# A second feed-forward product by one level of Strassen, with sums on GpSimd and three weight combinations streamed from DRAM

## The chip, the core and the metric

The kernel runs on one core of a Trainium2 chip. The metric is the device time in microseconds, as the median of several executions. A core has TensorE (PE; its weight loads, PEld, are listed apart), VectorE (DVE), ScalarE (ACT), GpSimd (POOL) and SyncE (SP), whose queue issues nearly all DMAs here. Each engine works through its instructions in the order of the program and waits on semaphores for the others.

## What is computed

An attention in which each query keeps its 32 largest scores, and behind it a feed-forward block, all in float32:

```python
# q, k, v: (8, 8, 576, 64); w_in: (512, 2048); w_out: (2048, 512)
scores = q @ k^T / 8
mask   = scores >= (the row's 32nd largest score)
attn   = softmax of the masked scores
x      = (attn @ v) with heads side by side     # 4608 tokens x 512
h      = x @ w_in
g      = h - tanh(h)
out    = g @ w_out                              # 4608 x 512
```

## The kernel before

**Attention.** A step handles two heads of one batch and a tile of 128 queries. Each batch has 16 such steps, and two more for the last 64 queries of each head; there are 144 steps in all. In step n, these parts of different steps run beside each other:

- `scores(n + 1)`: PE makes the scores in PSUM (L267), ACT copies them to SBUF (L275).
- `search(n)`: DVE finds the 32 largest (L297 to L319).
- `mask(n - 1)`: POOL makes the threshold `tb` (L334), ACT a Relu (L347), POOL a subtraction (L350) and flags (`bad`, L354). `expo(n - 1)`: ACT's exponential (L370), and POOL's small `rd` (L380).
- `invert(n - 2)` and `divide(n - 2)`: after the first round of the search, DVE's reciprocal (L389) and ACT's scaling (L396). `turn_z(n - 2)`: DVE transposes 32x32 blocks into `zx` when the search is done (L427).
- `spread_keys(n - 2)`, in steps whose pair of query tiles is complete (every second one): SP issues one DMA from `zx` to DRAM (`there`, L442), waits until it has landed and issues four DMAs back (`et`, L444).
- `values(n - 5)`: PE multiplies with v (L492), ACT copies the result to `xT` (L512).

The first batch (`pe`) transposes on PE instead, while the weights arrive in pieces and are converted on DVE, ACT and POOL.

**Feed-forward.** Tokens are gathered in units: 256 tokens (two query tiles of one batch), except 128 at the start of batch 0, and "rest" units of 128 tokens from two batches' last queries. `ffn(u)` cuts a unit into items. A full unit has 16 items `ffn_h` (256 columns times one block of 128 of `w_in`, four accumulated matmuls, L543; after every second item ACT makes tanh and a copy, L555 and L556, and POOL subtracts, L557) and 16 items `ffn_o` (two matmuls of 512 columns against `w_out`, L564; after eight of them ACT copies 128 tokens' output, L574, and SP stores it, L576). In the profile a float32 matmul is two records. A PSUM bank of `h_ps` holds 512 columns; there are two.

**The order.** The program is written out by hand. `rate()` computes how many items a step should take so that work lasts until the next unit is ready; `deal(part)` puts that share of them in place. A step's order, cut to what matters:

```python
mask(n - 1, exact)
search(n, exact, between)       # with invert, divide and turn_z of n - 2
spread_keys(n - 2)              # if steps[n - 2].last
deal(0.4)
due()                           # values
scores(n + 1)
expo(n - 1)
deal(0.2); deal(0.2)
for fn in todo.pop(n, []): fn() # loads of q, k, v
deal(0.2)
```

So SP meets a DMA that an item issues behind everything that the program issued on SP before it, the waits of `spread_keys` included.

Of the kernel before, what the change touches and what calls it, by code (L numbers as in the profile page):

```python
# [19 lines left out]
J = 4  # L20
# [5 lines left out]
class Step:  # L26
# [3 lines left out]

    def __init__(self, b, hp, qt, unit, col, i=0, nq=1, pe=False):
        self.b, self.hp, self.qt, self.unit, self.col = b, hp, qt, unit, col
        self.i, self.nq, self.pe = i, nq, pe
        self.rem = qt == J
        self.last = i == nq - 1

        self.lag = 2 if pe else LAG


class Unit:  # L40
# [3 lines left out]
    def __init__(self, blocks, tag):  # L44
        self.blocks, self.tag = blocks, tag
        self.n = 128 * len(blocks)
        self.xT = None
        self.g = []
# [3 lines left out]
def kernel(  # L52
# [46 lines left out]
    thpool = pool("th", 4)  # L99
    gpool = pool("g", 4)  # L100
    dpool = pool("d", 2, space=bass.MemoryType.DRAM)
    sc_ps = pool("sc_ps", 1, space=PS)
    zt_ps = pool("zt_ps", 2, space=PS)
    h_ps = pool("h_ps", 2, space=PS)

# [14 lines left out]
    et2 = [consts.tile([P, 4 * S], FP32, name="et")[:], later[:, 0 : 4 * S]]  # L120
    et_rem = later[:, 4 * S : 6 * S]
    e896 = consts.tile([P, 1], FP32, name="e896")
    nc.gpsimd.memset(e896[:], -896.0 * 2.0**23)
# [16 lines left out]
    def convert(piece, slot):  # L140
# [19 lines left out]

        e = h_ps.tile([P, NW], FP32, tag="h", name="e")[:] if j < WJ else f[:]
        nc.scalar.activation(e.bitcast(I32), fu, AF.Relu, bias=e896[:], scale=2.0**23)
# [14 lines left out]

    raw, kT, qT, vb, vr = {}, {}, {}, {}, {}

# [9 lines left out]

    def load_rows(name, b, hp, exact):  # L190

        if b == 0 and hp and not exact:
            x = early[2 * hp - 2 + (name == "q")]
        else:
            x = ldpool.tile([P, S], FP32, tag=f"{name}in", name=f"{name}in")[:]
        raw[name, b, hp] = x
        src = {"k": k, "q": q}[name]
        if b == 0 and hp and not exact:

            xv = x.rearrange("p (c t d) -> p t c d", t=2, d=D)  # L200
            for t in range(2):
                h = 2 * hp + t
                nc.sync.dma_start(
                    xv[:, t, 0:J, :], src[b, h, 0:JP, :].rearrange("(c p) d -> p c d", p=P)
                )
                nc.sync.dma_start(xv[0:R, t, J, :], src[b, h, JP:S, :])
            return
        for a in range(NG):
            h, d = 2 * hp + a // 2, a % 2 * G
            queue = nc.scalar if a and (name, b, hp, exact) == ("q", 0, 0, False) else nc.sync  # L210
            queue.dma_start(
                x[a * G : (a + 1) * G, :].rearrange("i (n d) -> i n d", d=G),
                src[b, h, :, d : d + G].rearrange("(n i) d -> i n d", i=G),
            )

    def load_v(b, hp):


        x = vb[b, hp] = kqpool.tile([P, 2, J, D], FP32, tag="vb", name="vb")
        y = vr[b, hp] = vrs[hp]  # L220
        for t in range(2):
            h, o = 2 * hp + t, t * R
            nc.sync.dma_start(
                x[:, t, :, :], v[b, h, o : o + JP, :].rearrange("(c p) d -> p c d", p=P)
            )
            o = 0 if t else JP
            nc.sync.dma_start(y[half(t), t, :], v[b, h, o : o + R, :])

    turned_pe = [True]

    def turn_rows(name, b, hp):

        d = kqpool.tile([P, S], FP32, tag=f"{name}T", name=f"{name}T")
        {"k": kT, "q": qT}[name][b, hp] = d
        x = raw.pop((name, b, hp))
        if not (b == 0 and hp and turned_pe[0]):
            nc.vector.transpose(d[:], x)  # L237
            return
# [19 lines left out]
    def scores(n):  # L258
        g = steps[n]
        ps = sc_ps.tile([P, 2, 2, 512], FP32, tag="sc", name="scps")  # L260
        for s in range(2):
            ks = slice(s * S2, (s + 1) * S2)
            for i in range(2 if g.rem else 1):
                qs = slice(JP, S) if g.rem else slice(g.qt * P, (g.qt + 1) * P)
                rows = half(i) if g.rem else slice(0, P)
                for t in range(2):
                    nc.tensor.matmul(  # L267
                        ps[rows, t, s, 0:S2],
                        qT[g.b, g.hp + i][half(t), qs],
                        kT[g.b, g.hp + i][half(t), ks],  # L270
# [128 lines left out]

    rxs = {}  # L400

    def spread(n):

        if steps[n].last:
            rd = rds.pop(n)
            nq = steps[n].nq
            rx = rxs[n] = xpool.tile([P, 2, 2, D], FP32, tag="rx", name="rx")
            nc.gpsimd.tensor_copy(
                rx[:, 0:nq], rd[:, 0:nq].unsqueeze(3).to_broadcast([P, nq, 2, D])
            )  # L410

    zxs, ets, last_et = {}, {}, [0]

# [18 lines left out]
    def spread_keys(n):  # L432
# [4 lines left out]
        if not rem:  # L437
            last_et[0] ^= 1
        et = ets[n] = et_rem if rem else et2[last_et[0]]
        w = steps[n].nq * S // 2  # L440
        there = dpool.tile([P, NG * w], FP32, tag=f"there{steps[n].nq}", name="there")
# [36 lines left out]
    def values(n):  # L478
# [7 lines left out]
        for i in range(2 if g.rem else 1):  # L486
# [3 lines left out]
            for c in range(J + 1):  # L490
                for t in range(2):
                    nc.tensor.matmul(  # L492
                        av[half(t), 0, cols],
                        vb[g.b, hp][:, t, c, :] if c < J else vr[g.b, hp][:, t, :],
                        es[:, :, (J + 1) * t + c if c < J else J].rearrange("p a i j -> p a (i j)"),
# [3 lines left out]
        if g.pe:  # L499
            rx = rxs.pop(n)  # L500
            for i in range(nq):
                nc.tensor.transpose(
                    in_order(av[:, 1, 0:w], nq)[:, i], rx[:, i].rearrange("p t d -> p (t d)"), ident[:]
                )
            xs = xrpool.tile([P, 2, N], FP32, tag="xs", name="xs")
            nc.scalar.copy(xs[:, :, 0:w], av[:, :, 0:w])
# [26 lines left out]
    def ffn_h(u, item):  # L533
# [3 lines left out]
        for f in range(item * per, (item + 1) * per):  # L537
            j, fo = f // FJ, (f % FJ) * P
            s = f * w % 512
            if s == 0:  # L540
                cur[u] = h_ps.tile([P, 512], FP32, tag="h", name="hps")
            for c in range(CD):
# [7 lines left out]
        if item % 2:  # L550
            th = thpool.tile([P, 512], FP32, tag="th", name="th")
            if item % 4 == 1:
                u.g.append(gpool.tile([P, 2, 512], FP32, tag="g", name="g"))
            g = u.g[-1][:, item % 4 // 2, :]
            nc.scalar.activation(th[:], cur[u][:], AF.Tanh)  # L555
# [3 lines left out]
    def ffn_o(u, i, part):  # L559
        if part == 0:  # L560
            cur[u] = h_ps.tile([P, DM], FP32, tag="h", name="ops")
        for f in range(2 * part, 2 * part + 2):
            o = f * u.n + i * P
            nc.tensor.matmul(  # L564
                cur[u][:],
                u.g[o // 1024][:, o % 1024 // 512, o % 512 : o % 512 + P],
                w_out[f // FJ][:, f % FJ, :],
# [7 lines left out]
        for rows, dst in u.blocks[i]:  # L575
            nc.sync.dma_start(dst, ot[rows, :])  # L576

    def ffn(u):

        nh = CF * u.n // (2 * P)  # L580
        for item in range(nh):
            f = (item + 1) * CF // nh - 1
            yield CD * (f // FJ + 1), u, lambda item=item: ffn_h(u, item)
        for i in range(len(u.blocks)):
            for part in range(CF // 2):
                yield CD * (WJ + part // 2 + 1), None, lambda i=i, part=part: ffn_o(u, i, part)

# [4 lines left out]
    def plan():  # L592
# [6 lines left out]
        for b in range(B):  # L599
            if b % 2 == 0:  # L600
                rest = Unit(
                    [[(half(i), out[(b + i) * S + JP : (b + i + 1) * S, :]) for i in range(2)]], "xTr"
                )
# [4 lines left out]
            for a, qts in enumerate(parts):  # L608
                unit = Unit([block(b, qt) for qt in qts], "xT")
                pe = b == 0  # L610
                for hp in range(NHP):
                    for i, qt in enumerate(qts):
                        steps.append(Step(b, hp, qt, unit, 0, i, len(qts), pe))
                    if hp == NHP - 1:
                        done[len(steps) - 1] = unit
                    if hp % 2 and a == (0 if b == B - 1 else len(parts) - 1):
                        steps.append(Step(b, hp - 1, J, rest, b % 2 * R, pe=pe))
                        if hp == NHP - 1 and b % 2:
                            done[len(steps) - 1] = rest
# [7 lines left out]
    def run(exact):  # L627
        plan()
        turned_pe[0] = not exact
        NS = len(steps)  # L630
        todo, at_round, turned = {}, {}, {}
# [4 lines left out]

        pairs = [(b, hp) for b in range(B) for hp in range(NHP)]
        for i, (b, hp) in enumerate(pairs):
            n = next(n for n, g in enumerate(steps) if (g.b, g.hp) == (b, hp))
            for x, name in enumerate("kq"):  # L640
                m = max(n - 5 + x, turned.get(name, -4))
                if b == 0 and not exact:
                    m = -4
                at(m, lambda x=(name, b, hp, exact): load_rows(*x))
                if x and i < NHP and not exact:
                    at(-4, lambda: load_piece())
                turn = lambda x=(name, b, hp): turn_rows(*x)
                if 0 < i < NHP:
                    at_round.setdefault((n - 1, 0), []).append(turn)
                    turned[name] = n - 1  # L650
                else:
                    at(n - 3 + x, turn)
                    turned[name] = n - 3 + x
            at(n + 1 if b else n - 1, lambda b=b, hp=hp: load_v(b, hp))

# [15 lines left out]
        def part(x, k):  # L671
            next(loaded[k][0])
            if x == 2:
                converted[0] = k + 1
                free.append(loaded[k][1])
                load_piece()
# [47 lines left out]
        def rate():  # L724


            have, low, high = len(work), 0.0, None
            coming = sorted((t, u.n // 8) for u, t in ready.items() if t > n)
            for t, k in coming + [(NS + LAG, 0)]:
# [108 lines left out]
```

## Time and profile before

| | |
|---|---|
| Median of three executions | 1509.0 us (1508.56 to 1510.21) |
| The profiled execution | 1509.65 us |
| Its span, first to last instruction | 1507.5 us |
| Mean granted TensorE clock | 0.982 |
| PE busy | 1426.5 us (95%), 7332 records |
| DVE busy | 1295.2 us (86%) |
| ACT busy | 1004.9 us (67%) |
| POOL busy | 879.1 us (58%) |
| DMA | 221.68 MB, queue of SP at 56.0% of 16 engines' time |

Busy times are unions over the span. The slices of the page cut the span into 40 equal parts; a digit is the busy share in tenths. The chain of waits follows the work that ended last back through what released it. In a group, the number behind the bar is its busy time, then the mean duration of one instruction, then the engine's idle time before them and what ended it.

### The profile page before, as it was taken

The numbers are of one execution on the slowest core, as the hardware profiler recorded it, in microseconds if no ns is written. First come the engines' busy times: TensorE is split into PE (matmuls) and PEld (weight loads), VectorE is DVE, ScalarE is ACT, GpSimd is POOL, SyncE is SP. The second block draws the span as 40 slices with busy tenths as digits, with TensorE's granted clock in tenths as the row PEclk, the third lists the DMA queues.
The fourth block names the chain that finished last, engine by engine and source line by source line (L and its number), as shares of the span: only waits on it lengthen the run. The fifth ranks groups of instructions, "written<-read, shape, count | busy, mean of one in ns | idle before, by whom it ended". The sixth has DMA issues, their size and how long they took to land.

```text
span 1507.5 us, 25020 instructions
## 1 busy us (share of the span) xinstructions
PE 1426.5 (95%) x7332; PEld 908.2 (60%) x7332; DVE 1295.2 (86%) x4886; ACT 1004.9 (67%) x1813; POOL 879.1 (58%) x1370
## 2 busy tenths in 40 slices
PE   4667898999999999999999999999999999999998
PEld 2454656465666565656565665657575675656673
DVE  7999899999998999999989999899988989886100
ACT  4766777777776777777676676768676676766220
POOL 3777667566565575657565575747474664646120
PEclk9888999999999999999999999999999999999999
DMA  9954123657854685567655865466554766443400
GB/s 277 373 170 167 25 43 92 171 156 153 205 147 140 164 166 156 134 176 171 162 136 146 175 147 165 138 166 159 156 145 117 174 144 177 111 140 105 109 7 17
DMA packets 248563, 221.68 MB, mean 147 GB/s; under 512 B 190816, under 2 KB 197984, under 8 KB 241248
## 3 DMA queue, kind: packets, MB, share of 16 engines
q1 hardware_dynamic: 246640, 219.75, 56.0%
q8 instruction: 61, 1.00, 0.3%
q14 instruction: 86, 0.70, 0.2%
q10 hardware_dynamic: 1776, 0.22, 0.1%
HBM read 136.17 MB, written 83.76 MB: 146 GB/s over the span
## 4 chain that ended last, share of the span: by engine, by line
PE 74%; DVE 15%; ACT 4%; POOL 2%; DMA 2%; issue 1%; SPq 0%; ACTq 0%; DVEq 0%; POOLq 0%
PE ops L564 28%; PE hps L543 28%; PE av L492 9%; PE scps L267 8%; DVE m L316 3%; DVE top L309 2%; DVE rest L319 2%; DVE zx L427 2%; DVE ab L303 1%; DMA w_in<-in_k_dram 1%; DVE f L170 1%; PE zt L464 1%; DVE f L159 1%; DVE top L319 1%; DVE ab L298 1%
## 5 line engine op out<-in xcount | busy, mean ns | idle before, releaser
L564 PE MATMUL ops<-w_out,g 128*128 128x512 f32 x1152 | 517.5, 600 | 2.4 <-POOL bad L354 1.5
L543 PE MATMUL hps<-xT,w_in 128*128 128x256 f32 (+1 forms) x2176 | 466.7, 372 | 1.0 <-ACT g L556 0.9
L350 POOL TENSOR_TENSOR z<-sc,z 128x576 f32<-128x576 f32 x288 | 404.5, 1426 | 86.2 <-ACT z L347 86.2
L543 PEld LDWEIGHTS hps<-xT,w_in 128*128 128x128 f32 x2176 | 392.0, 192 | 75.8 <-issue 21.6
L564 PEld LDWEIGHTS ops<-w_out,g 128*128 128x128 f32 x1152 | 213.3, 191 | 262.3 <-issue 250.3
L347 ACT ACTIVATE z<-sc,tb 128x576 f32<-128x576 f32 x288 | 207.6, 769 | 141.9 <-POOL tb L334 141.2
L557 POOL TENSOR_TENSOR g<-g,th 128x512 f32<-128x512 f32 x144 | 183.6, 1277 | 145.7 <-ACT g L556 140.9
L396 ACT ACTIVATE z<-z,rd 128x576 f32<-128x576 f32 x252 | 180.7, 764 | 97.0 <-DVE rd L389 96.9
L370 ACT ACTIVATE z<-z,nb 128x576 f32<-128x576 f32 x288 | 221.6, 774 | 2.5 <-POOL z L350 2.4
L380 POOL TENSOR_SCALAR rd<-den 128x2 f32<-128x2 f32 x144 | 32.7, 227 | 312.9 <-ACT z L370 307.1
L267 PE MATMUL scps<-kT,qT 64*128 64x288 f32 (+1 forms) x1280 | 189.0, 447 | 18.4 <-DVE qT L237 8.2
L427 DVE STREAM_TRANSPOSE zx<-z 128x1152 f32<-128x1152 f32 x126 | 172.0, 1365 | 35.2 <-ACT z L396 34.6
L309 DVE MAX8 top<-ab 128x8 f32<-128x144 f32 x864 | 194.6, 295 | 0.0
L275 ACT COPY sc<-scps 128x1152 f32<-128x1152 f32 x144 | 160.4, 1114 | 41.8 <-PE scps L267 41.4
L316 DVE MAX8 m<-rest 128x8 f32<-128x168 f32 x576 | 161.6, 322 | 0.0
L267 PEld LDWEIGHTS scps<-kT,qT 64*128 64x128 f32 (+1 forms) x1280 | 102.4, 184 | 94.5 <-issue 19.9
L316 DVE MAX8 m<-top 128x8 f32<-128x144 f32 (+1 forms) x576 | 151.7, 305 | 0.0
L555 ACT ACTIVATE th<-hps 128x512 f32<-128x512 f32 x144 | 84.2, 585 | 64.5 <-PE hps L543 62.1
L303 DVE TENSOR_TENSOR ab<-scps,sc 128x576 f32<-128x576 f32 x144 | 107.6, 748 | 0.0
L297 DVE TENSOR_TENSOR scps<-scps,sc 128x288 f32<-128x288 f32 x144 | 64.6, 449 | 46.1 <-ACT sc L275 45.7
L354 POOL TENSOR_SCALAR bad<-top,tb 128x3 uint8<-128x3 f32 x288 | 95.0, 341 | 0.0
L492 PE MATMUL av<-et,vb 128*64 128x256 f32 (+1 forms) x640 | 76.8, 372 | 18.2 <-ACT et L467 18.2
(78 smaller groups left out, 1536.8 us busy)
## 6 DMA issues: line engine op xcount, KB each, us to landing
there<-zx SPq DMA_DIRECT2D x56, 1152.0 KB, 4.2
spare<-there SPq DMA_DIRECT2D x112, 288.0 KB, 4.7
et<-there SPq DMA_DIRECT2D x112, 288.0 KB, 5.2
kin<-in_k_dram SPq DMA_DIRECT2D x116, 72.0 KB, 2.9
vb<-in_v_dram SPq DMA_DIRECT2D x64, 128.0 KB, 5.9
out_dram<-ot SPq DMA_DIRECT2D x32, 256.0 KB, 3.3
qin<-in_q_dram SPq DMA_DIRECT2D x113, 72.0 KB, 3.7
there<-zx SPq DMA_DIRECT2D x14, 576.0 KB, 5.2
```

The lines of the kernel that those rows point to most:

```text
L267: nc.tensor.matmul(ps[rows, t, s, 0:S2], qT[g.b, g.hp + i][half(t), qs], kT[g.b, g.hp + i][half(t), ks], start=True, stop=True,)
L309: nc.vector.max(top[:, t, o : o + 8], low[:, t, i, :])
L316: nc.vector.max(m[:, t, m8], seen[i][t])
L347: nc.scalar.activation(zv[:, t, :], scf[:, t, :], AF.Relu, bias=tb[:, t : t + 1], scale=-BIG)
L350: nc.gpsimd.tensor_tensor(zv[:, t, :], scf[:, t, :], zv[:, t, :], ALU.subtract)
L370: nc.scalar.activation(x["zv"][:, t, :], x["zv"][:, t, :], AF.Exp, bias=x["nb"][:, t : t + 1], scale=scale, accum_out=den[:, t : t + 1],)
L396: nc.scalar.activation(x, x, AF.Copy, scale=rds[n][:, g.i, t : t + 1])
L427: nc.vector.transpose(tiles(zx, g.nq)[:, :, :, g.i, :].rearrange("p c k j -> p k c j"), z[:].rearrange("p (k c j) -> p k c j", c=NG, j=G),)
L492: nc.tensor.matmul(av[half(t), 0, cols], vb[g.b, hp][:, t, c, :] if c < J else vr[g.b, hp][:, t, :], es[:, :, (J + 1) * t + c if c < J els ...
L543: nc.tensor.matmul(cur[u][:, s : s + w], w_in[j][:, c, fo : fo + P], u.xT[:, c, 0:w], start=(c == 0), stop=(c == CD - 1),)
L557: nc.gpsimd.tensor_tensor(g, g, th[:], ALU.subtract)
L564: nc.tensor.matmul(cur[u][:], u.g[o // 1024][:, o % 1024 // 512, o % 512 : o % 512 + P], w_out[f // FJ][:, f % FJ, :], start=(f == 0), sto ...
```

## The change

For a full unit, the second product becomes one level of Strassen's method in Winograd's form. With A the unit's 256 x 2048 `g` cut into 2 x 2 quarters (128 tokens by every second 128-block of the inner dimension) and B `w_out` cut likewise (1024 by 256), seven products of 128 x 1024 x 256 replace eight.

- **Products.** An item `ffn_p` is one half of a product's inner dimension: four matmuls of 256 columns. A full unit has 16 items `ffn_h` and 14 `ffn_p`, 30 instead of 32. Even products go to one PSUM bank, odd ones to the other, and accumulate there; after each product ACT copies 256 columns out, and the next product but one goes into the same place.
- **Sums.** Four sums of `g` quarters for each half of the inner dimension (eight of 128x512 elements) and three joins of outputs (128x256) a unit are made on POOL.
- **Weights.** Four combinations T1 to T4 for each of four parts of `w_out` are made once on POOL, two in each of the first eight items of the first full unit. B11, B22, T1 and T2 stay in SBUF. B21, T3 and T4 lie in DRAM (`kept`) and are streamed for each unit through `flow`, two buffers of 512 KB, one for each half of the inner dimension.
- **Other tiles.** To make room, q is loaded for each half of the query tiles, v is loaded twice a batch with three buffers instead of four, and several tiles share `more`.
- **Rest units** gather four batches' last queries (256 tokens) instead of two's, and so become full units.

The core of the diff:

```diff
+    ORDER = [("A11", "B11"), ("A12", "B21"), ("S2", "T2"), ("S3", "T3"), ("S1", "T1"), ("A22", "T4"), ("S4", "B22")]
+    FLOW = ["B21", "T3", "T4"]
+
+    def stream(i):
+        x, k = FLOW[i // 2], i % 2
+        nc.sync.dma_start(flow[k], kept[x][:, 4 * k : 4 * k + 4, :])
+
+    def sum_up(u, k, x):
+        (a11, a12), (a21, a22) = quarters(u, k)
+        s1, s2 = sums[k]
+        out_, a, b, op = [
+            (s1, a21, a22, ALU.add),
+            (s2, s1, a11, ALU.subtract),
+            (a21, a21, a11, ALU.subtract),
+            (a12, a12, s2, ALU.subtract),
+        ][x]
+        nc.gpsimd.tensor_tensor(out_, a, b, op)
...
+    def product(u, i, k):
...
+        acc = cur[u][i % 2][:, 0 : 2 * P]
+        fresh = i in (0, 1, 3)
+        for m in range(4):
+            if right in FLOW:
+                rhs = flow[k][:, m, :]
...
+            nc.tensor.matmul(acc, lhs[:, m, :], rhs, start=(fresh and k == 0 and m == 0), stop=(k == 1 and m == 3), skip_group_check=True)
+        return acc
+
+    def ffn_p(u, item):
+        i, k = item // 2, item % 2
+        acc = product(u, i, k)
...
+        if item in (3, 4):
+            sum_up(u, item - 3, 3)
+        if item < 3:
+            sum_up(u, 1, item)
+        if ORDER[i][1] in FLOW[:-1]:
+            stream(2 * FLOW.index(ORDER[i][1]) + 2 + k)
+        if not k:
+            return
+        if i == 0:
+            u.y = pair("oy")
+            nc.scalar.copy(u.y[:, lo], acc)
+        elif i == 1:
+            u.o0 = pair("ot")
+            nc.scalar.copy(u.o0[:, lo], acc)
+            join(u.o0[:, lo], u.y[:, lo])
...
+    def ffn_full(u, item):
+        ffn_h(u, item)
+        if item in (6, 7):
+            stream(item - 6)
+        if combined[0] < 4 * WJ:
+            for _ in range(2):
+                combine(combined[0] // 4, combined[0] % 4)
+                combined[0] += 1
+        if 8 <= item < 11:
+            sum_up(u, 0, item - 8)
...
-    gpool = pool("g", 4)
+    gpool = pool("g", 2)
...
-    h_ps = pool("h_ps", 2, space=PS)
+    h_ps = pool("h_ps", 1, space=PS)
...
-            if b % 2 == 0:
+            if b % 4 == 0:
                 rest = Unit(
-                    [[(half(i), out[(b + i) * S + JP : (b + i + 1) * S, :]) for i in range(2)]], "xTr"
+                    [
+                        [(half(i), out[(b + k + i) * S + JP : (b + k + i + 1) * S, :]) for i in range(2)]
+                        for k in (0, 2)
+                    ],
+                    "xTr",
                 )
...
-            at(n + 1 if b else n - 1, lambda b=b, hp=hp: load_v(b, hp))
+            at(n + 3 if b else n - 1, lambda b=b, hp=hp, part=part: load_v(b, hp, part))
```

## The prediction

> **What bounds the kernel now.** I read the page's busy shares and slices first, then the end of the chain of waits, the groups by form, and last the waits of the DMA queue.
>
> ```profile
> span 1507.5 us, 25020 instructions
> ...
> PE 1426.5 (95%) x7332; PEld 908.2 (60%) x7332; DVE 1295.2 (86%) x4886; ACT 1004.9 (67%) x1813; POOL 879.1 (58%) x1370
> ...
> PE   4667898999999999999999999999999999999998
> ...
> DVE  7999899999998999999989999899988989886100
> ...
> POOL 3777667566565575657565575747474664646120
> ```
>
> From the eleventh slice on PE is full, and it works 110 us longer than DVE: PE sets the end. It idles 1507.5 - 1426.5 = 81 us, nearly all in the first 300 us. But DVE is close behind: between 200 and 450 us the windows give it 246 of 250 us. There PE (242) waits for DVE.
>
> ```profile
> 581.67 7.06 PE ops L564 x16
> ...
> 592.21 7.10 PE hps L543 x32
> ...
> 1445.12 27.82 PE hps L543 x128
> 1472.95 27.48 PE ops L564 x64
> ```
>
> These are pieces of the chain (start, length, records). A 512-column record of the second product takes 7.06/16 = 0.441 us, a 256-column record 7.10/32 = 0.222: half the columns, half the time. So one item of the planner (4 records of 512 or 8 of 256) is 1.77 us of PE.
>
> ```profile
> SPq L444 <- DMA there<-zx: 274.3, 70, 5.3
> SPq L442 <- DVE zx L427: 242.0, 37, 18.4
> ```
>
> ```profile
> 748.89 0.34 SPq L442 DMA_DIRECT2D there<-zx  x1
> 753.11 1.76 SPq L444 DMA_DIRECT2D et<-there  x4
> 754.97 0.38 SPq L576 DMA_DIRECT2D out_dram<-ot  x1
> ```
>
> ```profile
> 737.86 5.35 PE ops L564 x12
> 743.20 1.73 PE hps L543 x8
> 744.93 1.17 PE scps L267 x8
> 746.10 7.10 PE hps L543 x32
> ```
>
> First two waits of SP's queue (us in total, times, longest), then its timeline, then the chain over the same time. SP issues in program order. In every second step it stands at L442 until DVE has turned zx, at the end of a search, then about 4 us at L444 until `there` has landed. The store of this block was ready when its last product ended, at 743.20 (plus the copy); it left at 754.97, 11.8 us later, when PE was five items on.
>
> **The change, part by part.**
>
> *Products.* 17 units of 256 tokens (14, one in batch 0, two rests) replace 64 records x 0.441 = 28.2 us by 7 x 8 x 2 = 112 records x 0.222 = 24.9. The two 128-token units keep 14.1 each. 36 x 14.1 = 508 becomes 17 x 24.9 + 28.2 = 451: -57. The first product of the rests goes from 128 columns (7.34 us for 64 records, 0.115 each; 512 of them, 59) to 256 columns (256 x 0.222 = 57): -2. Together **-59** on the path: from 300 us on PE has 12 us of idle time, so PE time counts one to one.
>
> The Trainium skill's page "TensorE: Matmul & The Clock Gate" (Part 3, The mechanism) says that a weight load overlaps running matmuls only if its row group differs. The trace differs: 128 records with 128x128 loads of 0.192 us follow each other every 0.217 us. By the page 48 more loads a unit would cost 9.2 us a unit and the change would lose 100 us on PE alone; the row decides.
>
> *Sums on GpSimd.* Each unit adds 8 x 1.277 us (row g<-g,th, the same 128x512) and three joins of 256 columns at 0.729 (row xT<-xs): 12.4 us. POOL goes from 879 to 879 + 17 x 12.4 + 16 x 1.28 (weight combinations) = 1110 us of about 1400, 79%. It lies beside PE, but in POOL's order: behind a sum wait tb, z and rd of the attention, behind these ACT's Relu and, at its end, the score copy that DVE's next search needs. From tb to the end of the next score copy lie 0.3 + 2 x 0.77 (Relu) + 2 x 0.76 (division) + 1.11 = 4.5 us, so tb may start 8.8 - 4.5 = 4.3 us after DVE's step; the timeline has it at 2 to 3 in the mean. A step gets 12.4/8.5 = 1.5 us more POOL work; part falls into the 2.1 us a step that POOL now waits for rd (307 us in all). Cost between 0 and 0.5 us in each of the 55 DVE-bound steps, 28 us; I take +5, since slack remains.
>
> *The 16 combinations* come in eight items of the first full unit, two each: 20 us of POOL where the windows give it 34 to 40 of 50 already. Up to +20, down to 0; I take +10.
>
> *Rests over four batches.* Their items come at batch 4 and batch 8 instead of after each second batch. By the planner's rule the steps 20 to 75 get about 3.15, later 3.4 items instead of 3.4 and 3.75; with 2.5 us of scores and values PE needs 8.2 and 8.5 us a step where DVE's step is 8.78. PE idles 0.6 x 25 + 0.25 x 31 = 23 us there against 11 now: up to +12, 0 if other stalls lie in the same place. +5.
>
> *Split q and repeated v loads*: 28 more transposes at 0.11 us (737 ns for 576 elements, 1365 for 1152) are 3 us of DVE: +1. The some 130 q and 56 v DMAs are on SP, which is the next point. Seven copies of 0.367 for two of 0.574 add 1.4 us a unit to ACT at 67%: nothing.
>
> *Streams.* `flow` has one buffer for each half of the inner dimension. T3's half may be issued only when product item 2 (or 3) has read B21's, and is needed at item 6 (7); T4's follows item 6 (7) and is needed at 10 (11). So from release to need PE has three items, 5.3 us, and one set of scores (1.2) or scores and values (3.5): 6.5 to 8.8 us, 7.7 in the middle. In that time SP must come to the DMA and 512 KB must land. Landing: 3.7 us (w_out, 512 KB) to 6.3 (stores issued right behind et); 4.6 is the middle (spare, 512 KB). How late SP comes is what the stores show, issued in the same deals: of the 29 between 289 and 1344 us the delays from last matmul to issue are 15.0, 9.0, 8.7, 7.1, 0.6, 0.6, 2.5, 6.5, 7.3, 1.7, 10.7, 1.8, 11.8, 0.6, 10.5, 3.7, 11.0, 9.1, 7.7, 2.5, 10.5, 8.8, 0.6, 12.2, 3.5, 3.9, 10.2, 8.0, 0.6: 6.4 in the mean, 14 over 7.5, 12 under 4. In the example above, a stream in the store's place would land at 754.97 + 4.6 = 759.6 and be needed two items after 746.10, at 749.7: 9.9 us of PE standing. Over the 29 delays, max(0, delay + 4.6 - 7.7) is 3.9 us in the mean; 15 units lie among steps with such transposes, two hand-overs each: 30 x 3.9 = 116.
>
> A second way: half of the steps turn zx, and 0.4 of the items are dealt ahead of the scores; the first deal of such a step holds one of a hand-over's two halves in about a third of the cases, 10 of 30, at some 8.5 us; some 12 fall into its later deals (SP 5 us late, 1.5 us of stall), the rest cost nothing: 103. A PE stall isn't regained: it delays the scores, thus DVE, thus SP by as much, and the lag is there again. It fills idle time where DVE binds, so I take **+95**; bounds 30 (landing 3.7, only the ten) and 150 (landing 6.3).
>
> The skill's page "DMA: Bandwidth & Descriptors" (Anatomy of one DMA) fits 2.0 us + bytes/436 GB/s, 3.2 us for 512 KB, for GpSimd's queue. No row here is as short for this size; by it the streams would cost about 30 us less.
>
> *Other new waits*: product i + 2 waits for ACT's copy of product i (3.55 us later at least; ACT now starts a tanh 1.2 us after its bank in the median, 3.6 at the 95th percentile), and item 1 for the last g (3.6 us in the median, 3.1 us of PE before it): +6, between 0 and 20.
>
> **Sum.** 1507.5 - 59 + 5 + 10 + 5 + 1 + 95 + 6 = 1570.5 us of span. The profiled execution took 1509.65, 2.15 more than its span and 0.65 above the median of 1509.0: 1570.5 + 2.15 - 0.65 = 1572.
>
> **The rivals.** (1) *Streams in time, faster*: the 12 stores under 4 us speak for it, and DMA queues that are 56% busy; the longer half of the delays speaks against. Then 1509 - 59 + 27 = 1477. It decides where stalls stay under 59 - 27 = 32 us, 1.1 us a hand-over. Chance 0.18, 1450 to 1500. (2) *GpSimd sets the pace*: ACT's 141 us of waits for tb speak for it, 21% of free POOL time against. Streams in time, 55 steps at 9.3 instead of 8.78: 1477 + 28 - 5 = 1500, spread 1490 to 1520. Chance 0.10. With late streams it is the upper end of my forecast. (3) *No gain in the products* since 256-column records don't run at half time: excluded by the chain's rows as far as they go; it is in the upper end too.
>
> **Numbers.** Forecast (late streams): 0.72, 1500 to 1650 for itself. About 3 us (0.2%) can be told from no change. Faster 0.18 + 0.02 of (2) + 0.01 of the forecast's lower edge = 0.21; same 0.03; slower 0.76. The range reaches down into the first rival, to 1488, and up to 1632 (1572 plus 55 for the streams' upper bound and 5 of the other terms): some 0.12 below, 0.07 above.
>
> **What would show it.** Right: PE busy near 1367 but the span up; in the waits, the product line on PE waiting for flow's DMA, 60 to 140 us in some 20 to 35 places, up to 12 us each; DVE idle more, on ACT's score copy; POOL about 1110 us; product records near 0.222 us in the chain. Wrong: those waits under 30 us in all; or PE waiting for POOL's sums instead; or SP's issue of flow within 3 us of the product that frees it.

## The result, and the profile after

The changed kernel takes 1724.9 us (1722.9 to 1728.9, four executions) against 1509.6 for the kernel before, run beside it: a ratio of 1.1425, 95% interval 1.1396 to 1.1454. The direction of the forecast held, its size did not: +215 us instead of +63, and outside the range. The page of the changed kernel, with the lines that answer to those shown of before, and with the granted clock:

```profile
span 1724.6 us, 27027 instructions
...
PE 1440.0 (83%) x7892; PEld 1085.6 (63%) x7892; DVE 1299.3 (75%) x4914; ACT 1017.6 (59%) x1898; POOL 1103.7 (64%) x1573
...
PE   4677986896987979797969798979796988788998
...
DVE  7998977989797979797968878779696886684000
...
POOL 4776787676584857575757656767666584756434
PEclk9788998899898989898989999989898999899999
...
PE 29%; DVE 24%; DMA 16%; ACT 14%; POOL 10%; issue 4%; SPq 2%; DVEq 0%; ACTq 0%; POOLq 0%
```

Before, the rows of the clock and of the chain were:

```profile
PEclk9888999999999999999999999999999999999999
...
PE 74%; DVE 15%; ACT 4%; POOL 2%; DMA 2%; issue 1%; SPq 0%; ACTq 0%; DVEq 0%; POOLq 0%
```

PE is no longer full from the eleventh slice on: nines and sevens alternate. Its idle time went from 81 to 1724.6 - 1440.0 = 285 us. DVE dips in the same slices. The clock, at nine tenths or more in before from the fifth slice to the end, now loses a tenth in every second or third slice; the mean is 0.925 instead of 0.982. In the chain of waits PE held 74% of the span; now it holds 29%, and DMA 16% instead of 2%.

The waits of PE (us in total, times, longest):

```profile
PE hy L721 <- DMA more<-keptT: 132.5, 23, 12.7
PE scps L329 <- DVE top L367: 37.5, 13, 12.2
...
PE hps L607 <- ACT g L620: 15.8, 12, 2.7
PE hx L721 <- POOL g L621: 8.6, 7, 3.2
```

and of SP's queue:

```profile
SPq L508 <- DMA there<-zx: 282.2, 70, 6.5
SPq L506 <- DVE zx L490: 207.1, 33, 15.1
...
SPq L701 <- PE hy L721: 84.2, 20, 29.3
```

The first line is the forecast's main wait: products (L721) stand for T3 and T4 (`more<-keptT`). One of these hand-overs in the timeline of PE (start, length, engine, line, names, records; in brackets the idle time before it and what ended it):

```profile
593.47 3.72 PE L721 MATMUL hy<-more,g 128*128 128x256 f32 x16
597.02 3.82 PE L721 MATMUL hx<-w_out,more 128*128 128x256 f32 x16
600.77 1.95 PE L556 MATMUL av<-et,vb 128*64 128x256 f32 x16
602.55 0.60 PE L556 MATMUL av<-et,vr 128*64 128x256 f32 x4
603.08 1.24 PE L329 MATMUL scps<-kT,qT 64*128 64x288 f32 x8
611.04 5.42 PE L721 MATMUL hy<-more,g 128*128 128x256 f32 x16 [6.72 <-DMA more<-keptT]
```

and in that of SP's queue over the same time:

```profile
597.50 0.35 SPq L506 DMA_DIRECT2D there<-zx  x1
602.07 1.74 SPq L508 DMA_DIRECT2D spare<-there  x4
603.91 0.85 SPq L701 DMA_DIRECT2D more<-keptT  x2
604.81 0.97 SPq L276 DMA_DIRECT2D vb<-in_v_dram  x2
605.88 5.80 SPq L259 DMA_DIRECT2D qin<-in_q_dram  x4
```

Items 2 and 3 had read B21's halves at 595.5 and 597.2. SP issued `there` at 597.50, stood until it had landed, and came to the two streams only at 603.91; they landed some 7 us later, beside other loads. PE ran out of work at 604.3 and began again at 611.04. Then the same sixteen records took 5.42 us instead of 3.72. The windows say why (length; busy PE, PEld, DVE, ACT, POOL; granted clock; DMA share; GB/s):

```profile
590.00:600.00 10.00, 8.69 (x41) 6.51 (x40) 9.66 (x38) 6.09 (x12) 8.93 (x12) 1.00 0.55 130
605.50:611.00 5.50, 0.00 (x0) 0.00 (x0) 5.38 (x13) 3.12 (x8) 3.77 (x8) 0.70 1.04 280
611.00:618.00 7.00, 6.96 (x24) 5.72 (x24) 3.78 (x22) 1.50 (x3) 0.37 (x1) 0.75 0.78 200
```

While PE stood, its clock was taken down, and for half of the 7 us after it came back it was still at half rate.

### The profile page after: what moved, and what is told of

Its sections match the earlier page's. It is cut to its first block, busy times and chain, and to the rows that moved or that the text cites. A ratio compares the mean times of both kernels' runs of the same rounds, so it can differ in the third digit from the quotient of the medians.

```text
span 1724.6 us, 27027 instructions
## 1 busy us (share of the span) xinstructions
PE 1440.0 (83%) x7892; PEld 1085.6 (63%) x7892; DVE 1299.3 (75%) x4914; ACT 1017.6 (59%) x1898; POOL 1103.7 (64%) x1573
## 4 chain that ended last, share of the span: by engine, by line
PE 29%; DVE 24%; DMA 16%; ACT 14%; POOL 10%; issue 4%; SPq 2%; DVEq 0%; ACTq 0%; POOLq 0%
PE hps L607 9%; PE hy L721 7%; DMA more<-keptT 6%; DMA there<-zx 5%; PE hx L721 5%; DVE m L378 4%; ACT z L458 4%; DVE top L371 4%; ACT z L409 3%; PE av L556 3%; PE scps L329 3%; POOL g L621 3%; DVE zx L490 3%; DVE rest L381 2%; DVE ab L365 2%
## 5 line engine op out<-in xcount | busy, mean ns | idle before, releaser
L607 PE MATMUL hps<-xT,w_in 128*128 128x256 f32 (+1 forms) x2176 | 475.4, 375 | 15.3 <-ACT g L620 14.4
L721 PE MATMUL hy<-more,g 128*128 128x256 f32 x816 | 233.6, 445 | 144.2 <-DMA more<-keptT 132.5
L721 PEld LDWEIGHTS hy<-more,g 128*128 128x128 f32 x816 | 178.6, 225 | 195.1 <-issue 125.2
L329 PE MATMUL scps<-kT,qT 64*128 64x288 f32 (+1 forms) x1120 | 163.6, 441 | 38.2 <-DVE top L367 36.7
L359 DVE TENSOR_TENSOR scps<-scps,sc 128x288 f32<-128x288 f32 x144 | 64.6, 448 | 147.8 <-ACT sc L337 147.7
L329 PEld LDWEIGHTS scps<-kT,qT 64*128 64x128 f32 (+1 forms) x1120 | 89.2, 182 | 94.2 <-issue 30.3
L721 PE MATMUL hx<-w_out,g 128*128 128x256 f32 x544 | 132.4, 390 | 16.7 <-POOL g L621 8.6
L721 PEld LDWEIGHTS hx<-w_out,g 128*128 128x128 f32 x544 | 101.3, 192 | 43.6 <-POOL g L621 16.1
L721 PE MATMUL hx<-w_out,more 128*128 128x256 f32 x544 | 126.9, 383 | 0.0
```

Source lines behind the costliest of these rows:

```text
L329: nc.tensor.matmul(ps[rows, t, s, 0:S2], qT[g.b, g.hp + i, g.part][half(t), qs], kT[g.b, g.hp + i][half(t), ks], start=True, stop=True,)
L607: nc.tensor.matmul(cur[u][:, s : s + w], w_in[j][:, c, fo : fo + P], u.xT[:, c, 0:w], start=(c == 0), stop=(c == CD - 1),)
L721: nc.tensor.matmul(acc, lhs[:, m, :], rhs, start=(fresh and k == 0 and m == 0), stop=(k == 1 and m == 3), skip_group_check=True)
```

## The experiments

Where a kernel leaves out something, its expectation says what. "Without reloads" means that T3 and T4 are not streamed; B21 still is.

### Is it the reloads, the sums or the layout?

`plain_layout` keeps the change's tiles, loads and rest units, and the second product of before (16 items `ffn_o`); it has no streams, sums or combinations.

```diff
-        self.items = 16 if self.n == 128 else 30
+        self.items = 16 if self.n == 128 else 32
...
-        for item in range(2 * len(ORDER)):
-            yield 2 * WJ * CD, None, lambda item=item: ffn_p(u, item)
+        for i in range(2):
+            for part in range(CF // 2):
+                yield 2 * WJ * CD, None, lambda i=i, part=part: ffn_o(u, i, part)
```

> The changed kernel's tiles, loads, rest units and plan, but the second product as before (eight pairs of 512-column matmuls a block, nothing streamed, no weight combinations, no sums). If the waits for streamed weights are the cause (theory W): 1500 to 1530 us, since the layout alone costs little. If the sums on GpSimd are the cause (theory S): the same. If the regrouped rests and the repeated q and v loads cost much (theory L): over 1550.

Measured: 1523.8 us, ratio 1.0098 (1.0069 to 1.0128): the layout alone costs some 14 us.

`no_reload`:

```diff
-        if ORDER[i][1] in FLOW[:-1]:
-            stream(2 * FLOW.index(ORDER[i][1]) + 2 + k)
```

> The changed kernel without the loads of T3 and T4: the three products read what the first load left, which leaves those two combinations out of the computation. W: waits and half clock go, PE busy near 1367 us, 1450 to 1510 us. S: over 1600, since all sums are still there.

Measured: 1560.8 us, ratio 1.0344 (1.0308 to 1.0380). This lies between the two ranges: the reloads are the greater part of the loss, but not all of it.

`no_sums` (the sums and the joins):

```diff
-        nc.gpsimd.tensor_tensor(out_, a, b, op)
+        return
...
-        lhs = {"A11": a11, "A12": a12, "A22": a22, "S1": sums[k][0], "S2": sums[k][1], "S3": a21, "S4": a12}[left]
+        lhs = {"A11": a11, "A12": a12, "A22": a22, "S1": a21, "S2": a22, "S3": a21, "S4": a12}[left]
...
-            nc.gpsimd.tensor_tensor(a, a, b, ALU.add)
+            return
```

> The changed kernel without the eight sums and three joins of a unit on GpSimd (left out of the computation; S1 and S2 are replaced by g's quarters), streams as they are. W: waits for flow stay at 110 to 150 us, 1640 to 1725 us. S: under 1600.

Measured: 1692.0 us, ratio 1.1213 (1.1133 to 1.1292); PE still waits 145.2 us for T3 and T4.

`products_alone` is both edits together.

> The changed kernel without the loads of T3 and T4 and without the sums and joins (all left out of the computation): the seven products, the layout and the combinations of weights stay. The kernel with sums but without these loads took 1561 us. If GpSimd's sums are what is left above the kernel before (theory P): 1455 to 1490 us, PE busy near 1367. If the layout, the combinations or the products' own waits are (theory Q): over 1530.

Measured: 1523.9 us, ratio 1.0097 (1.0068 to 1.0126), again between the ranges of the two theories. The reloads cost 1725 - 1561 = 164 us with the sums and 1692 - 1524 = 168 without; the sums 33 with the reloads and 37 without. So the parts nearly add.

`plain_stream` puts the hand-over alone into `plain_layout`: for a unit's first 128 tokens half of `w_out`'s blocks come through `flow`, for the second a quarter, freed and needed at the same distance of items.

```diff
+        use = full and (i, part) in ((0, 2), (0, 3), (0, 6), (0, 7), (1, 2), (1, 3))
...
-                w_out[f // FJ][:, f % FJ, :],
+                wide[part % 2][:, f % 2, :] if use else w_out[f // FJ][:, f % FJ, :],
...
+        if use and i == 0:
+            stream(3 if part < 4 else 1, part % 2)
```

> As the kernel with the layout alone, but a quarter of w_out's rows (the same values) comes through the two flow buffers, in the same items 2, 3, 6, 7, 10 and 11 of the second product and with the same release as in the changed kernel; no Strassen, no sums. W: the hand-over alone brings the loss, PE waits 110 to 150 us for flow's DMA, runs some 70 us longer at half clock, 1680 to 1760 us. S: waits for the DMA only take the place of others, under 1600.

Measured: 1710.3 us, ratio 1.1334 (1.1272 to 1.1396). The page's busy times and clock, and the first of PE's waits:

```profile
PE 1478.4 (86%) x7076; PEld 915.4 (53%) x7076; DVE 1297.3 (76%) x4914; ACT 1006.2 (59%) x1813; POOL 880.2 (51%) x1370
...
PEclk9687998898989899998989999989898989899999
```

```profile
PE ops L633 <- DMA more<-keptw: 140.6, 20, 14.8
```

Without Strassen and without any added work on POOL, the hand-over costs 1711.9 - 1521.4 = 190.5 us of span. Of this 140.6 are waits, and 47.0 are PE's busy time (1431.4 in `plain_layout`) at the same 7076 records. Together 187.6. The clock makes most of the second part: PE's busy time inside half-clock stretches of the trace rises from 73 to 147 us, and half of that difference is 37 us. So the same records at a slower clock are a fifth to a quarter of the loss.

### What makes the hand-over late?

`plain_stream_8` has eight items from a load's release to its need instead of four, and one hand-over a unit instead of two. The edit is shown against `plain_stream`.

```diff
-        use = full and (i, part) in ((0, 2), (0, 3), (0, 6), (0, 7), (1, 2), (1, 3))
+        use = full and (i, part) in ((0, 2), (0, 3), (1, 2), (1, 3))
...
-            stream(3 if part < 4 else 1, part % 2)
+            stream(1, part % 2)
```

> The kernel with the layout and plain products, one hand-over a unit instead of two, with eight items between release and need instead of four: flow is read in items 2 and 3, loaded anew, and read again in items 10 and 11. If the loss comes from too little time between release and need (theory W): PE waits under 15 us for flow, 1520 to 1545 us (1524 without streams, 1710 with two hand-overs over four items). If any hand-over of 512 KB on SyncE's queue costs some 90 us a kernel, whatever its lead (theory H): about 1610.

Measured: 1539.3 us, ratio 1.0184 (1.0155 to 1.0214); 9.3 us of waits in four places, PE busy 1439.6. Halving the hand-overs alone would have left some 95 of 190 us; 16 are left. The distance decides.

`spread_late` moves `spread_keys`, SP's standing place, behind the deals; `small_stream` loads a quarter of T3 and T4 (128 KB).

```diff
-            if here(-2) and not pe and steps[n - 2].last:
-                spread_keys(n - 2)
...
             deal(0.0 if pe else 0.2)
+            if here(-2) and not pe and steps[n - 2].last:
+                spread_keys(n - 2)
```

> The changed kernel, whole, with one block of the step moved: spread_keys stands behind the third deal instead of ahead of the first, so the queue of SP meets most of a step's streams ahead of the wait for zx. If the queue's order makes the streams late (theory W1): the waits for flow fall from 132 us to under 60, most streams are issued within 2 us of the product that frees their buffer, 1590 to 1640 us. If the landing of 512 KB in a busy DMA system does (W2): waits over 100 us, 1680 or more.

```diff
-        nc.sync.dma_start(flow[k], kept[x][:, 4 * k : 4 * k + 4, :])
+        n = 4 if i < 2 else 1
+        nc.sync.dma_start(flow[k][:, 0:n, :], kept[x][:, 4 * k : 4 * k + n, :])
```

> The changed kernel, but T3 and T4 are loaded with one quarter of each half (128 KB instead of 512; the rest of the buffer keeps what it held, so those combinations are left out in part). If SyncE's late issue makes most of the wait (W1): waits for flow 70 to 100 us, 1640 to 1680. If the landing of 512 KB and the traffic do (W2): waits under 50 us, under 1620.

Measured: 1671.5 us (1.1074, 1.1042 to 1.1107) and 1685.1 us (1.1149, 1.1114 to 1.1185). PE's waits for the streams fall from 132.5 to 100.0 and 100.3. In the first SP issues 3.6 us in the mean after the product, instead of 4.8; in the second the transfers land in 3.2 us in the median, instead of 5.8. `spread_late` falls between the ranges of W1 and W2, `small_stream` a little above that of W1. Neither edit takes the waits away, but `spread_late` took away only a quarter of SP's lag (37 of the 68 streams were issued within 2 us, instead of 24), so it does not try the queue's order to the end; its transfers also land sooner, in 4.7 us. Lag and landing together come to 10.5 us in the mean in the changed kernel, 8.5 in `spread_late` and 8.1 in `small_stream`.

### Can another queue carry them?

`act_queue` issues the streams on ACT's queue; `late_and_act` has `spread_late`'s edit too.

```diff
-        nc.sync.dma_start(flow[k], kept[x][:, 4 * k : 4 * k + 4, :])
+        nc.scalar.dma_start(flow[k], kept[x][:, 4 * k : 4 * k + 4, :])
```

> The changed kernel, whole, with the streams issued from ScalarE's queue instead of SyncE's. W1: issued some 1 to 5 us after the product (ACT's own lag), waits for flow 30 to 80 us, 1590 to 1660 us; ACT pays by waiting for products. W2: waits over 100 us, 1680 or more.

> Both edits in one. W1: no better than the better of the two by more than 20 us, since either takes the streams out from behind the wait for zx. W2: over 1680 us.

Measured: 1640.6 us (1.0870, 1.0826 to 1.0913) and 1630.6 us (1.0803, 1.0762 to 1.0844). In `act_queue` the streams are issued 0.8 us after the product in the mean and land in 4.8 in the median, together 6.0 in the mean: the lag is nearly gone, and PE's waits for the streams fall to 15.0 us. But those for DVE's search rise to 95.2 (37.5 in the changed kernel). DVE's waits show what DVE waited for:

```profile
DVE zx L490 <- DMA there<-zx: 76.5, 20, 7.3
DVE zx L490 <- ACT z L458: 73.0, 33, 15.9
DVE qT L296 <- DMA qin<-in_q_dram: 31.1, 10, 6.2
```

The first stood at 9.0 us in the changed kernel. So 70 to 80 us over `no_reload` remained with hardly a wait for a stream. The next two kernels ask whether that is the bytes, ACT's own order, or the second queue. In `traffic_alone` (SP's queue) and `act_traffic` (ACT's) the same four transfers a unit go to DRAM and nobody waits for them. The edit is made in the changed kernel; shown is that of `act_traffic`, and `traffic_alone` has `nc.sync` throughout:

```diff
+    aside = [keep.tile([P, 4, 2 * P], FP32, name=f"aside{i}") for i in range(4)]
...
-        nc.sync.dma_start(flow[k], kept[x][:, 4 * k : 4 * k + 4, :])
+        dst = flow[k] if i < 2 else aside[i - 2][:]
+        (nc.sync if i < 2 else nc.scalar).dma_start(dst, kept[x][:, 4 * k : 4 * k + 4, :])
```

> The kernel without reloads of T3 and T4 (1561 us), with the same four DMAs of 512 KB a unit in the same places of SyncE's queue, but from DRAM to DRAM and with nobody waiting for them. If this traffic delays the other transfers (theory T, for the 70 us by which the kernel with streams on ScalarE's queue and a late spread_keys, whose waits for flow are only 13 us, lies above 1561): 1600 to 1640. If the rest comes from waits in ScalarE's and SyncE's order: 1555 to 1575.

> The kernel without the reloads of T3 and T4, but at the places of its reloads the same four 512 KB transfers a unit go from DRAM to DRAM, issued on ACT's queue; nobody waits for them and they wait for no product (the products use what stands in `flow`). The same on SP's queue gave 1567, none 1561. Theory C (two queues hold up each other's transfers): DVE's waits for `there` and `qin` rise as with the reloads on ACT's queue (76 and 31 us there, 24 in all with the transfers on SP's queue), and the time comes to 1590 to 1630. Theory A (with the reloads on ACT's queue, ACT stands at each DMA until the product has read the buffer, and what is behind it in ACT's order is late): nothing waits here, so the time stays at 1560 to 1572 and the wait for `there` under 30 us.

Measured: 1567.4 us (1.0370, 1.0340 to 1.0400) and 1613.9 us (1.0684, 1.0666 to 1.0702). Against `no_reload` the bytes cost 4 to 7 us (by the ratios and by the medians); on ACT's queue they cost 51 to 53. SP's waits in `act_traffic`:

```profile
SPq L508 <- DMA there<-zx: 301.0, 70, 9.0
...
SPq L259 <- DMA aside<-keptT: 80.7, 19, 11.4
...
SPq L276 <- DMA aside<-keptT: 27.1, 7, 7.3
```

and the one line of this kind at L259 in `traffic_alone`:

```profile
SPq L259 <- DMA aside<-keptT: 12.6, 12, 1.9
```

All lines of this kind together are 145.6 us in `act_traffic` and 13.9 in `traffic_alone`. SP's loads of q (L259) and v (L276) and its `there` stand until a transfer on the other queue has landed, though they neither read nor overwrite `aside`. The transfers themselves were no slower (5.5 us to landing in the median, 6.3 on SP's queue), so the price that theory C gave is right and its reason, slower transfers, is not: it is SP's issue that is held. With it DVE's waits for `there` and `qin` rise from 24.1 and 2.7 us to 63.8 and 17.3.

The records of the trace name the tie: it is in the program. Each of the 1144 DMAs counts its landing on one of eight semaphores, whichever queue issues it, and none is issued before the previous DMA on its semaphore has landed. All of the 36 waits that make up the 145.6 us end when the `aside` transfer lands whose semaphore SP's next DMA carries. Eleven of them began before ACT had even issued that transfer (37 us in all). A kernel with semaphores of their own for the second queue wasn't run. ACT also spends 36 us on issuing the 68 transfers, and how much of the cost that makes wasn't separated.

### Where did the products' gain go, and what do the sums cost?

`no_joins` leaves out the three joins in `no_reload`:

```diff
-            nc.gpsimd.tensor_tensor(a, a, b, ALU.add)
+            return
```

> The kernel without reloads of T3 and T4 and without the three joins of a unit on GpSimd (both left out of the computation); the eight sums stay. 1561 us with sums and joins, 1524 without both. If the work itself counts: 11 x 8/10 of the 37 us stay with the sums, 1550 to 1558. If a join that waits for ScalarE's copy holds up GpSimd's queue (43 us of such waits in the profile): 1525 to 1540.

Measured: 1550.6 us, ratio 1.0259 (1.0230 to 1.0289). This is the lower edge of the range for the work itself. The joins are 36 of the 203 us of sums and joins on POOL (18%) and 10 to 13 of the 37 us (by the medians and by the ratios). That is more than their share, but the greater part of the loss stays with the sums of `g`. ACT's wait for POOL's threshold, in `products_alone`:

```profile
ACT z L409 <- POOL tb L396: 146.4, 98, 12.0
```

and in `no_reload`:

```profile
ACT z L409 <- POOL tb L396: 253.7, 120, 12.0
```

The sums stand ahead of `tb` in POOL's order; ACT's Relu, division and score copy follow it, and DVE's wait for ACT's z rises by 35.4 us, from 47.5 to 82.9. The span rises by 34.7.

`no_combos` leaves the 16 combinations out of `products_alone`:

```diff
-            for _ in range(2):
-                combine(combined[0] // 4, combined[0] % 4)
-                combined[0] += 1
+            combined[0] += 2
```

> The kernel without reloads, sums and joins (1524) and also without the 16 weight combinations on POOL and their stores; the products then use the quarters as they are. Theory D (the combinations' stage costs some 15 us and the steps in which DVE has no slack take the rest of the products' gain): 1507 to 1514. Rival E (the combinations cost nothing, all of the gain goes where DVE sets the pace): 1520 to 1525.

Measured: 1506.9 us, ratio 0.9963 (0.9943 to 0.9983): the combinations cost 17 to 20 us. Between 200 and 300 us PE is busy for 79.7 us in `products_alone` and 94.3 here. With reloads, sums, joins and combinations all gone, the change is worth a third of a per cent. The windows from 300 to 800 us, before:

```profile
300.00:800.00 500.00, 493.68 (x2506) 308.58 (x2505) 480.29 (x1839) 360.94 (x647) 307.20 (x489) 1.00 0.65 160
```

and in `no_combos`:

```profile
300.00:800.00 500.00, 471.67 (x2711) 357.32 (x2708) 489.18 (x1888) 368.66 (x682) 307.93 (x496) 0.99 0.74 181
```

DVE is busy 98% of this half millisecond: PE's saved time became PE's idle time. From `plain_layout` to `no_combos` PE's busy time falls by 42.8 us and its idle time rises by 26.5: 12.1 between 300 and 800 us, and 14.5 from there to 1380. The end moves by 16.3.

No variant that does the whole computation beats the kernel before.

## Why the prediction was wrong

Measured by the spans of the profiled executions, each step of the sum against the pair of kernels that differ in it (the five executions of `no_combos` lie within 7 us, so the first row is good to a few us):

| step | predicted | measured | from |
|---|---|---|---|
| products, rests, transposes, other new waits | -59 + 5 + 1 + 6 = -47 | -2.4 | `no_combos` 1505.1 - before 1507.5 |
| combinations | +10 | +17.9 | `products_alone` 1523.0 - 1505.1 |
| sums and joins | +5 | +34.7 | `no_reload` 1557.7 - 1523.0 |
| streams | +95 | +166.9 | after 1724.6 - 1557.7 |
| together | +63 | +217.1 | |

The sum misses by 154 us. The streams' term is 72 of it, the step from PE time to span in the products 45, the sums' term 30, the combinations 8.

**Streams.** Right: place, cause and number of the waits. 132.5 us in 23 places, up to 12.7, answer to "60 to 140 us in some 20 to 35 places, up to 12 us each", the longest a little above. The landing, taken as 4.6 us, was 5.8 in the median, but SP's lag, taken as 6.4 in the mean, was 4.8, so that the two together were about as forecast. The page "DMA: Bandwidth & Descriptors" of the Trainium skill (Anatomy of one DMA), which the prediction weighed, gives 3.2 us for this size on GpSimd's queue; on SP's queue the runs lie still further from it than the rows of before. Here lies the first step that failed: the sum took the 103 to 116 us of waits down to +95, though nearly all of the waits went into the span, and it put at nothing what a wait does to the clock. From `no_reload` to after PE's busy time rises by 42.3 us (1397.7 to 1440.0) at the same 7892 records. By the clock's records 33 of these are the clock: the busy time inside half-clock stretches rises from 92 to 158 us, and half of the difference is lost. 132.5 + 42.3 - 11.1 (less waiting for DVE's search, 48.6 to 37.5) = 163.7 of the 166.9. After 300 us the changed kernel has 25 stretches at half clock, each a multiple of 3.4 us long but for the last, which the end cuts off; before has one, at its very end. In the traces of the changed kernel, `plain_stream` and `no_reload`, 44 of the 45 gaps of at least 2.7 us on PE are followed by such a stretch, of which 3 to 8 us lie behind the gap, when PE works again; of the 21 gaps between 0.8 and 1.2 us one is. The skill's page "TensorE: Matmul & The Clock Gate" (Part 1, What's actually happening) says as much: the clock is halved after an idle window of about 3.4 us and freed after a busy one. The traces agree on the length of the stretches; but 8 of the 9 gaps of 2.7 to 3.4 us, shorter than the page's window, were followed by one as well. The prediction cited another part of that page and priced its waits without this one. The row was there in before, too: a clock of 0.98 is the clock of a PE that hardly ever stops.

**Products.** "From 300 us on PE has 12 us of idle time, so PE time counts one to one" is the second step that failed. For PE time that is taken away the next engine decides, and DVE was busy for 480 of the 500 us already. Its share was in the prediction's own first part, and the sum did without it. The products took 43 us from PE's busy time, not 57, and 16 from the end. The records explain most of the 14 between 43 and 57. The records of the second product alone fall by 48 us from `plain_layout` to `no_combos`, and 15 us of them lie at half clock in `no_combos` against 4, which costs some 6; without that they would have saved 54, and the last unit's product items took 24.3 us, near the 24.9 forecast. The other 5 us are spread over PE's other records. The rests and the other tiles cost 13.9 (`plain_layout` 1521.4) instead of -2 + 5 + 1 = 4: PE's idle time between 300 and 800 us rises from 6.3 to 16.3, 10 of the 12 given as the bound, and PE's busy time by 5.

**Sums.** The mechanism was in the prediction, the second rival's, and so was its bound of 28 us; +5 "since slack remains" was the wrong choice within it, and 34.7 lies above it. The slack was in the mean of POOL's time, not in the places between a sum and the `tb` behind it: ACT's wait for `tb` rose by 107 us. Whether DVE bound more steps than the 55 of that bound wasn't counted; in `products_alone` it is busy for 98% of the time from 300 to 800 us and for 92% of the 580 us behind.

**Combinations.** 17.9 lies within the 0 to 20 given, near the upper end, where POOL has nothing free.

**What was to be seen.** POOL 1104 (forecast 1110), the product line's waits for flow's DMA, and DVE waiting for ACT's score copy (147.7 us in 50 places) came as told. PE's busy time did not: 1440 against 1367, by the clock and the smaller saving. The first rival, streams in time at 1477, would have failed even with the streams in time: `no_reload` has 1561.

## What to carry to other kernels

Price a saving on the busiest engine by the second busiest engine's free time in the same stretch, not by the first one's idle time. In these traces a PE wait of about 3 us or more cost its length and then left 3 to 8 us of work at half clock. One buffer that is reloaded between uses needs a cover of the worst delay of its queue plus the landing, not of the mean: eight items from release to need instead of four, with half the hand-overs, took 190 us of loss down to 16. Work put on an engine with 40% free time still costs where it stands in order ahead of something that a bound engine needs.

## What the runs showed of the hardware that was not expected

- PE's records between waits ran at half clock in stretches of 3.4 us and its multiples, 25 of them behind 300 us in the changed kernel. For the same 7892 records PE was busy 42 us longer, 33 of them by the clock.
- Moving four 512 KB transfers a unit from SP's queue to ACT's, with nobody waiting for them, cost 1613.9 - 1567.4 = 46 us: SP's own DMAs waited 145.6 us for transfers that they shared no data with, since the program's DMAs of both queues share eight landing semaphores.
- POOL's 203 us of sums left DVE's operations as long as they were: the 576-element add took 748 ns before and 747 in `no_reload`. No contention between the two engines shows; the loss is order.
